# A fused attention and gated-convolution kernel: part of an output product moved ahead in the sixth chunk, the single tile's value product spread over two steps, and its convolution taps and gating moved later

## The chip, the cores and the metric

The kernel runs on one core of one Trainium2 chip. The metric is the device time in microseconds (us) of one execution; a kernel's time is the median of several. The engines are named as the profile names them: PE is the matmul engine (PEld its weight loads), DVE the vector engine, ACT the scalar engine, POOL GpSimd, SP the queue that issues most DMAs. Each works through its own instructions in order, and waits on semaphores for the others.

## The reference

Eight batches of 3200 rows with 256 features; z has 64. In short:

```python
scores = z @ z.T / S                    # per batch, S = 3200
attn = relu(scores) ** 2
x = u * (attn @ v)
gate = sigmoid(sum(conv_w[k] * x shifted down by 4 - k rows, k = 0..4))
out = (gate * (x @ w_val)) @ w_out
```

All in float32. The kernel splits each operand into a high part in the engine's reduced format and the rest, so that each product is three matmuls: low by high, high by low, high by high.

## The kernel before

**Tiles and steps.** A batch has 25 tiles of 128 rows: six chunks of four tiles (512 columns, `c` = 0 to 5 in the code, so the sixth chunk is `c` = 5) and a single tile at the end. The work of a batch is a list of 81 steps. A step takes one pair of key tiles for one chunk: its scores are computed three steps ahead on PE (`scores`, into a PSUM bank pair `s`), ACT squares them and casts the high part (`ah`, L643 to L646), DVE subtracts for the low part (`al`, L652), and then `attend` multiplies with v and adds into the chunk's two accumulator banks `acc`. Half of the pairs of scores are not computed but fetched, turned, from a copy in DRAM (`mirrored`, tile `m`). A chunk has 13 steps, the sixth has 16.

**Two row halves.** `side_by_side` (L426) runs two matmuls at once, each on 64 of PE's 128 rows, one writing bank 0 and the other bank 1. So a product is a list of pairs of matmuls, and it has two parts: in part 1 the halves change banks. At the start of part 1 `turn_round` puts a no-op on PE that waits for the last matmul of part 0, since the other half wrote these banks. `attend(…, 0)` and `attend(…, 1)` are the two parts of a step; scores or another product (a "fill") usually stand between them.

**Behind the attention.** When a chunk's last `attend` is done, DVE multiplies both `acc` banks with u (`gated`, L766, two instructions), which frees the banks for the next chunk. In the next chunk follow the convolution, the sigmoid, the value product (`value`, w_val, banks `misc0` and `misc1`), and one chunk later the output product (`project`, w_out, the same two `misc` banks, allocated anew each time, one buffer each). `project` stands at the first step of a chunk. In the sixth chunk its part 1 is cut into three pieces of two pairs: one in step 0, one each in steps 1 and 2.

**The single tiles.** They are handled in five groups of batches: (0, 1), (2, 3), (4, 5), (6), (7). In batches 0 to 7 their products with v (`swap`) fill steps of the sixth chunk. The rest of the work on the first four groups is put in the batch after the group, at step numbers counted from its start `s0`: taps of the convolution in `one_conv` (L1148 on ACT, L1150 on DVE), `one_sigmoid`, `one_value` (w_val, banks `misc0` and `misc1` too), `one_gated` (L1239, DVE reads both `misc` banks; two instructions), `one_gated_high` (L1243), `one_gated_low` (L1247), and at `s0` + 48 `one_project`. Step `s0` + 38 is the last of the third chunk, and step `s0` + 39 the first of the fourth.

**What sets the order.** The order is written by hand. For each step the loop at the end of the function issues PE's work, then, at a chunk's last step, `gated`, then what `at_step` put there, in the order of the calls. `fill_at` puts work between the two parts of a step.

Of the kernel before, what the change touches and what calls it, by code (L numbers as in the profile page):

```python
# [17 lines left out]
def attn_glu_kernel(  # L18
# [216 lines left out]
    def has_copy(b, c, i=None):  # L235


        if i is not None and place[b, c, i] >= NP - 2 and has_copy(b, c + 1):
            return False
        return c < n_chunks - 1 and b > 0  # L240
# [17 lines left out]
    def tiles(c, i):  # L258

        return (GROUP * i, GROUP) if c == ONE else pairs[i]  # L260
# [61 lines left out]
    def start(b, c):  # L322

        c = min(c, n_chunks - 1)
        return starts[b, c] if b < B else N
# [92 lines left out]
    def side_by_side(upper, lower):  # L418


        ins = None
        for i in range(max(len(upper), len(lower))):
            for r, mms in zip(rows, (upper, lower)):
                if i < len(mms):
                    out_, st, mv, first, last = mms[i]
                    ins = nc.tensor.matmul(out_, st[r], mv[r], start=first, stop=last)  # L426
        return ins
# [27 lines left out]
    def s_bank():  # L455

        if held_s[0] is None:
            next_s[0] = 1 - next_s[0]
            x = 1 - next_s[0]
        else:  # L460
            x = 1 - held_s[0]
        return ps.tile([P, 2, 512], F32, name=f"s{x}", bufs=1)

    def scores(b, c, i, terms=range(3)):
        if not terms:
            return
        k, n = tiles(c, i)
        w = sizes[c] * P
        if (b, c, i) not in st_:
            st_[b, c, i] = s_bank()  # L470
        s = st_[b, c, i]

        q = zt[b, c][:, :, :w].rearrange("p x (t a r) -> p x a t r", t=sizes[c], r=BLK)
        if has_copy(b, c, i):
            q = zq[b, c][:, :, :w].rearrange("p x (a y) -> p x a y", a=P // BLK)
        if halves(b, c, i):
            q, w = q[:, :, :, 2 * BLK :] if has_copy(b, c, i) else q[:, :, :, 2:], w // 2
        a = P // BLK
        sides = []
        for j in range(2):  # L480
            g, t = homes[k + (0 if n == 1 else j)]
            ks = slice(t * P, (t + 1) * P)
            qs = slice(j * (a // 2), (j + 1) * (a // 2)) if n == 1 else slice(0, a)
            kk = zt[b, g]
            mms = []
            for m in terms:
                kp, qp = (((0, 0), (0, 1), (1, 0)) if b == c == i == 0 else ((0, 1), (1, 0), (0, 0)))[m]
                mms.append((s[:, j, : w // 2 if n == 1 else w], kk[:, kp, ks], q[:, qp, qs], m == 0, m == 2))
            if both(c, i):
                for m in terms:  # L490
                    kp, qp = ((0, 1), (1, 0), (0, 0))[m]
                    q1 = zt[b, ONE][:, qp, j * (P // 2) : (j + 1) * (P // 2)]
                    mms.append((s[:, j, w // 2 : w // 2 + P // 2], kk[:, kp, ks], q1, m == 0, m == 2))
            sides.append(mms)
        side_by_side(*sides)

    def both(c, i):
        return c == n_chunks - 1 and i == SINGLE
# [7 lines left out]
    def halves(b, c, i):  # L506
        return two_pairs(b, c) and i == own(c, 1)
# [452 lines left out]
    def project(b, c, part, piece=0, pieces=1):  # L960
        if part == piece == 0:
            pos[b, c] = [ps.tile([P, 512], F32, name=f"misc{x}", bufs=1) for x in range(DH)]
        sides = [project_list(b, c, x, part == 0, part == 1) for x in (part, 1 - part)]
        turn_round("misc", cut(sides, piece, pieces), part and piece == 0)
# [352 lines left out]
    def at_step(s, fn, *args, first=False):  # L1317
        work = todo.setdefault(min(s, END), [])
        work.insert(0 if first else len(work), (fn, args))

    def fill_at(s, fn, *args):
        filling.setdefault(s, []).append((fn, *args))
# [38 lines left out]
    )  # L1361
    V_HIGH = (7, 8, 9, 10, 11, 12, 13, 16, 17, 18, 14, 15, 19)

    CONVERSIONS = (
        (2, 2, convert_conv(), 10),
        (13, 4, convert("val"), 10 + 2 * LAG["val"]),
# [2 lines left out]
    for b in range(B):  # L1369
        for c in range(n_chunks + 1):  # L1370
            s0 = start(b, c)
# [23 lines left out]
            if (b, c) != LAST:  # L1395
# [7 lines left out]
                ends = project_places(nb, nc_)  # L1403
# [40 lines left out]
    for g, members in enumerate(GROUPS[:-1]):  # L1444
        s0 = start(members[-1] + 1, 0)
        at_step(s0 + 6, one_load, g)
        at_step(s0 + 9, one_mul, g)
        fill_at(s0 + 24, one_turn, g)
        at_step(s0 + 24, one_halo, g)
        at_step(s0 + 24, one_place, g)  # L1450
        at_step(s0 + 25, one_high, g)
        at_step(s0 + 26, one_low, g)
        for h in range(DH):
            for k in range(KW):
                at_step(s0 + 26 + 4 * h + max(k - 1, 0), one_conv, g, h, k)
        at_step(s0 + 34, one_sigmoid, g)
        for part in range(2):
            fill_at(s0 + 37, one_value, g, part)
        for e in range(DH):
            at_step(s0 + 37, one_gated, g, e)  # L1460
        at_step(s0 + 38, one_gated_high, g)
        at_step(s0 + 39, one_gated_low, g)
        for part in range(2):
            fill_at(s0 + 48 + part, one_project, g, part)
        at_step(s0 + 49, one_out, g)
    g, s0 = len(GROUPS) - 1, start(*LAST)
# [8 lines left out]
    at_step(9, fetch_weights, "out", w_out, "zq")  # L1475
    for first, step, fn, n in CONVERSIONS:
        for j in range(n + 1):
# [5 lines left out]
    with tc.manual_schedule():  # L1483
# [13 lines left out]
        for s in range(min(todo), END + 1):  # L1497
            b, c, i = steps[s] if s >= 0 else (0, 0, 0)
            cm, p = position(s)[1:] if s >= 0 else (0, s)
            ahead = steps[s + AHEAD] if 0 <= s + AHEAD < N and s != -1 else None  # L1500
            late = steps[AHEAD - 1] if s == 0 else None
            places, ends = (value_places(b, cm), project_places(b, cm)) if s >= 0 else ((), ())
            piece = PIECES[len(places)][places.index(p)] if p in places else None
            terms = [] if lacks(s) or not ahead else list(range(3))
            if s in FILL:
                no_wait(zeros[:, :P], zeros, "misc1", FILL[s])
            k = b * n_chunks + cm if s >= 0 else 0
            before = divmod(k - 2, n_chunks) if k >= 2 and p == project_at(b, cm) else None
# [3 lines left out]
            if s >= WHOLE_FROM:  # L1512
                assert not left and not terms and not piece and not before
                if s < END:
                    for h in range(DH):
                        attend_whole(b, c, i, h)
                        if s == WHOLE_FROM and h == 0:
                            one_turn(len(GROUPS) - 1)
            else:
                fill, whole = [], False  # L1520
                if before and ends:
                    project(*before, 0)
                    scores(*ahead, terms)
                    terms, fill = [], [(project, *before, 1, 0, len(ends) + 1)]
                elif before:
                    project(*before, 0)
                    scores(*ahead, terms[:1])
                    project(*before, 1)
                    terms = terms[1:]
                if p in ends:  # L1530
                    fill = [(project, *divmod(k - 2, n_chunks), 1, 1 + ends.index(p), len(ends) + 1)]
                if piece:
                    fill = [(value, *behind, *piece)]
                    behind = None
                fill += filling.get(s, [])
                if s >= NP and p == 0 and not before:

                    scores(*ahead, terms)
                    for h in range(DH):
                        attend_whole(b, c, i, h)  # L1540
                    terms, whole = (), True
                elif s >= 0 and c != ONE:
                    attend(b, c, i, 0)
                if late:
                    scores(*late)
                    attend(b, c, i, 1)
                    whole = True
                if s == -AHEAD:
                    scores(*ahead, terms)
                    z_turn(0, 1)  # L1550
                    terms = []
                if behind:
                    value(*behind, 0)
                if terms:
                    scores(*ahead, terms)
                for fn, *args in fill:
                    fn(*args)
                if s >= 0 and not whole and c != ONE:
                    left.append((b, c, i))
                if terms or fill or behind or s + 1 == WHOLE_FROM:  # L1560
                    for n in range(len(left)):
                        attend(*left.pop(0), 1, again=n > 0)
                if behind:
                    value(*behind, 1)
# [19 lines left out]
            if s == END:  # L1584

                b, c = LAST
                g = len(GROUPS) - 1
# [104 lines left out]
```

## Time and profile before

| | |
|---|---|
| time, median of 3 runs | 2253.08 us (2252.02 to 2254.63) |
| time of the profiled execution | 2252.91 us |
| its span, first to last instruction | 2251.1 us |
| PE busy | 2242.5 us, 100% of the span |
| DVE, ACT, POOL busy | 1855.5 us (82%), 1700.1 us (76%), 84.6 us (4%) |
| granted clock of PE | 1.00 |

The span is what the trace covers; the execution's own time has 1.8 us around it. An engine is counted as busy while an instruction runs on it, and matmul ends are modelled, so that PE's share is no measure of how densely matmuls start. The steps of a stretch are compared by the starts of their matmuls.

### The profile page before, as it was taken

Reading aid. Unit: us, or ns where it says so; the run is one execution under the profiler, and the core shown is the slowest. Engines: PE = TensorE matmul, PEld = TensorE weight load, DVE = VectorE, ACT = ScalarE, POOL = GpSimd, SP = SyncE. Lnnn points to the kernel's source line nnn. Section 1 sums busy time; section 2 is a strip of 40 time slices with the busy share of each in tenths; the row PEclk is TensorE's granted clock in tenths of the full one; section 3 lists DMA queues with packets and bytes.
Section 4 is the critical chain, followed back from the end, with each engine's and each line's share of the span. In section 5 each row is a group of like instructions: output and inputs, shape, how many; then the busy total and the mean of one; then the engine's idle time right before and its main releaser. Section 6 shows DMA issues by size and latency. Waiting matters only on the chain.

```text
span 2251.1 us, 49980 instructions
## 1 busy us (share of the span) xinstructions
PE 2242.5 (100%) x20283; PEld 1915.8 (85%) x20283; DVE 1855.5 (82%) x2290; ACT 1700.1 (76%) x2136; POOL 84.6 (4%) x128
## 2 busy tenths in 40 slices
PE   9999999999999999999999999999999999999999
PEld 7788988889888998888888889888888888988888
DVE  7988788877889778887888968888788887888777
ACT  8986688766887668876698766987669776697764
POOL 0000000000000000000000000000000000000001
PEclk9999999999999999999999999999999999999999
DMA  6558857887677876788777786778868778577663
GB/s 155 113 140 206 213 140 165 191 184 197 159 167 177 190 193 155 174 186 187 179 171 169 188 188 171 170 176 184 208 142 189 175 179 205 144 186 174 169 180 101
DMA packets 702423, 390.79 MB, mean 174 GB/s; under 512 B 410608, under 2 KB 635888, under 8 KB 702192
## 3 DMA queue, kind: packets, MB, share of 16 engines
q1 hardware_dynamic: 701376, 387.21, 73.1%
q8 instruction: 158, 2.59, 0.5%
q14 instruction: 73, 0.60, 0.1%
q10 hardware_dynamic: 816, 0.39, 0.1%
HBM read 213.92 MB, written 173.54 MB: 172 GB/s over the span
## 4 chain that ended last, share of the span: by engine, by line
PE 97%; DVE 2%; ACT 1%; issue 0%; DMA 0%; DVEq 0%; ACTq 0%
PE acc L426 71%; PE s L426 13%; PE misc L426 12%; DVE al L652 0%; DVE turned L518 0%; PE acc L736 0%; PE misc L731 0%; ACT a L643 0%; ACT a L644 0%; DVE gate L814 0%; PE acc L731 0%; DMA z_rows<-in_z_dram 0%; PE misc L201 0%; DVE x L766 0%; ACT ah L646 0%
## 5 line engine op out<-in xcount | busy, mean ns | idle before, releaser
L426 PE MATMUL acc<-ah,v_hl 64*128 64x512 f32 x9472 | 1610.2, 388 | 0.8 <-DVE x L766 0.7
L426 PEld LDWEIGHTS acc<-ah,v_hl 64*128 64x128 f32 x9472 | 948.0, 184 | 160.8 <-issue 1.9
L426 PE MATMUL acc<-al,v_hl 64*128 64x512 f32 x4736 | 968.1, 387 | 0.1
L426 PEld LDWEIGHTS acc<-al,v_hl 64*128 64x128 f32 x4736 | 483.9, 184 | 77.8 <-DVE al L652 1.3
L652 DVE TENSOR_TENSOR al<-a,ah 128x1024 fp32r<-128x1024 f32 x342 | 393.0, 1149 | 175.0 <-ACT ah L646 173.7
L643 ACT ACTIVATE a<-s 128x1024 f32<-128x1024 f32 x342 | 328.9, 962 | 132.0 <-PE s L426 118.8
L646 ACT CAST ah<-m 128x1024 fp32r<-128x1024 f32 x258 | 269.3, 1047 | 168.0 <-PE acc L426 90.9
L644 ACT ACTIVATE a<-a 128x1024 f32<-128x1024 f32 x342 | 343.5, 1004 | 10.8
L652 DVE TENSOR_TENSOR al<-m,ah 128x1024 fp32r<-128x1024 f32 x258 | 312.4, 1211 | 36.1 <-ACT ah L646 33.4
L646 ACT CAST ah<-a 128x1024 fp32r<-128x1024 f32 (+1 forms) x320 | 316.8, 990 | 10.2
L518 DVE STREAM_TRANSPOSE turned<-a 128x1024 f32<-128x1024 f32 (+1 forms) x282 | 323.1, 1146 | 0.2 <-DMA mir<-turned 0.2
L814 DVE SCALAR_TENSOR_TENSOR gate<-x,cw,gate 128x512 f32<-128x512 f32 (+1 forms) x392 | 285.4, 728 | 4.3 <-ACT gate L812 0.5
L426 PE MATMUL s<-zq,zhl 64*128 64x512 f32 (+1 forms) x1596 | 223.4, 378 | 0.0
L426 PEld LDWEIGHTS s<-zq,zhl 64*128 64x128 f32 x1596 | 154.6, 184 | 27.2
L766 DVE TENSOR_TENSOR x<-acc,ut 128x512 f32<-128x512 f32 (+1 forms) x96 | 61.4, 680 | 77.6 <-PE acc L426 64.7
L818 ACT ACTIVATE gate<-gate 128x512 f32<-128x512 f32 (+1 forms) x98 | 61.0, 622 | 65.7 <-DVE gate L814 65.3
L916 ACT CAST gvh<-gv 128x512 fp32r<-128x512 f32 x94 | 58.3, 620 | 50.2 <-DVE gv L912 49.6
L912 DVE TENSOR_TENSOR gv<-misc,gate 128x512 f32<-128x512 f32 x94 | 64.5, 686 | 21.2 <-PE misc L426 17.0
L426 PE MATMUL misc<-xh,w_val_lo 64*128 64x512 f32 x376 | 77.3, 387 | 0.1
L426 PE MATMUL misc<-xl,w_val_hi 64*128 64x512 f32 x376 | 77.2, 386 | 0.0
L426 PE MATMUL misc<-xh,w_val_hi 64*128 64x512 f32 x376 | 77.2, 386 | 0.0
L426 PE MATMUL s<-v_hl,ah 64*128 64x512 f32 x400 | 76.2, 394 | 0.0
(199 smaller groups left out, 2025.6 us busy)
## 6 DMA issues: line engine op xcount, KB each, us to landing
mir<-turned SPq DMA_DIRECT2D x468, 256.0 KB, 4.1
m<-mir SPq DMA_DIRECT2D x234, 512.0 KB, 5.0
u_raw<-in_u_dram SPq DMA_DIRECT2D x384, 64.0 KB, 3.7
mir<-turned SPq DMA_DIRECT2D x376, 64.0 KB, 2.3
m<-mir SPq DMA_DIRECT2D x94, 256.0 KB, 4.6
out_dram<-ob SPq DMA_DIRECT2D x152, 128.0 KB, 3.5
v_raws<-in_v_dram SPq DMA_DIRECT2D x100, 128.0 KB, 6.4
z_raw<-in_z_dram SPq DMA_DIRECT2D x180, 64.0 KB, 3.3
```

What stands on the lines that cost most here:

```text
L426: ins = nc.tensor.matmul(out_, st[r], mv[r], start=first, stop=last)
L518: nc.vector.transpose(into[:, t : t + m], a[:, j * w : (j + m) * w].rearrange("p (t m x) -> p t m x", t=m, x=BLK))
L643: nc.scalar.activation(a[:, : n * w].rearrange("p (j x) -> p j x", j=2), s[:, :, :each], AF.Relu, scale=scale)
L644: nc.scalar.activation(a, a, AF.Square)
L646: nc.scalar.copy(hi, a)
L652: nc.vector.tensor_tensor(lo, a, f32(hi), op=ALU.subtract)
L766: nc.vector.tensor_tensor(x[:, h, HALO + cols.start : HALO + cols.stop], accs[b, c][h][:, cols] if with_ is None else with_, ut[b, c][:, h ...
L814: nc.vector.scalar_tensor_tensor(g, tap, cw[:, h, k : k + 1], g, op0=ALU.mult, op1=ALU.add)
L818: nc.scalar.activation(g, g, AF.Sigmoid)
L912: nc.vector.tensor_tensor(gv[:, :w], pvs[b, c][e][:, :w], gates[b, c][:, e, :w], op=ALU.mult)
L916: nc.scalar.copy(gvs[b, c][0][:, e, :w], gv_[b, c, e][:, :w])
```

## The change

The output product's first piece of part 1 moves, in the sixth chunk, from between the two parts of the first `attend` to ahead of both. The single tile's value product, both parts at `s0` + 37, now has part 0 at `s0` + 37 and part 1 at `s0` + 38; `one_gated`, `one_gated_high` and `one_gated_low` move from 37, 38, 39 to 38, 39, 40. The taps stand at a table `ONE_CONV` of steps, and the sigmoid one step later.

```diff
--- before.py
+++ after.py
@@ -1360,6 +1360,8 @@
         (16, (18, 19, 24), None),
     )
     V_HIGH = (7, 8, 9, 10, 11, 12, 13, 16, 17, 18, 14, 15, 19)
+
+    ONE_CONV = ((0, 0, 1, 2, 4), (4, 5, 6, 7, 8))
 
     CONVERSIONS = (
         (2, 2, convert_conv(), 10),
@@ -1452,14 +1454,14 @@
         at_step(s0 + 26, one_low, g)
         for h in range(DH):
             for k in range(KW):
-                at_step(s0 + 26 + 4 * h + max(k - 1, 0), one_conv, g, h, k)
-        at_step(s0 + 34, one_sigmoid, g)
+                at_step(s0 + 26 + ONE_CONV[h][k], one_conv, g, h, k)
+        at_step(s0 + 35, one_sigmoid, g)
         for part in range(2):
-            fill_at(s0 + 37, one_value, g, part)
+            fill_at(s0 + 37 + part, one_value, g, part)
         for e in range(DH):
-            at_step(s0 + 37, one_gated, g, e)
-        at_step(s0 + 38, one_gated_high, g)
-        at_step(s0 + 39, one_gated_low, g)
+            at_step(s0 + 38, one_gated, g, e)
+        at_step(s0 + 39, one_gated_high, g)
+        at_step(s0 + 40, one_gated_low, g)
         for part in range(2):
             fill_at(s0 + 48 + part, one_project, g, part)
         at_step(s0 + 49, one_out, g)
@@ -1520,8 +1522,11 @@
                 fill, whole = [], False
                 if before and ends:
                     project(*before, 0)
-                    scores(*ahead, terms)
-                    terms, fill = [], [(project, *before, 1, 0, len(ends) + 1)]
+                    if terms:
+                        scores(*ahead, terms)
+                        terms, fill = [], [(project, *before, 1, 0, len(ends) + 1)]
+                    else:
+                        project(*before, 1, 0, len(ends) + 1)
                 elif before:
                     project(*before, 0)
                     scores(*ahead, terms[:1])
```

**The first step of the sixth chunk, PE** (batch 0; the other seven are alike). `misc` are the output product's banks, `acc` the accumulators that the product with v (`ah`, `al` by `v_hl`) fills, `s` the bank of `swap`. Before:

```order
L426 MATMUL misc_3380<-gvh,w_out_hi 128x512
L426 MATMUL acc_3393<-ah,v_hl_714 128x512 [waits DVE_49,Activation_49]
L426 MATMUL acc_3394<-ah,v_hl_714 128x512 [waits DVE_49]
L426 MATMUL acc_3393<-al,v_hl_714 128x512
L426 MATMUL acc_3394<-al,v_hl_714 128x512
L426 MATMUL acc_3393<-ah,v_hl_714 128x512
L426 MATMUL acc_3394<-ah,v_hl_714 128x512
L426 MATMUL misc_3380<-gvh,w_out_lo 128x512 [waits PE_49]
L426 MATMUL misc_3379<-gvh,w_out_lo 128x512
L426 MATMUL misc_3380<-gvl,w_out_hi 128x512
L426 MATMUL misc_3379<-gvl,w_out_hi 128x512
L426 MATMUL s_3406<-v_hl_714,ah 128x512 [waits PE_49]
```

After:

```order
L426 MATMUL misc_3380<-gvh,w_out_hi 128x512
L426 MATMUL misc_3380<-gvh,w_out_lo 128x512 [waits PE_49]
L426 MATMUL misc_3379<-gvh,w_out_lo 128x512
L426 MATMUL misc_3380<-gvl,w_out_hi 128x512
L426 MATMUL misc_3379<-gvl,w_out_hi 128x512
L426 MATMUL acc_3398<-ah,v_hl_714 128x512 [waits DVE_49,Activation_49]
L426 MATMUL acc_3399<-ah,v_hl_714 128x512 [waits DVE_49]
L426 MATMUL acc_3398<-al,v_hl_714 128x512
L426 MATMUL acc_3399<-al,v_hl_714 128x512
L426 MATMUL acc_3398<-ah,v_hl_714 128x512
L426 MATMUL acc_3399<-ah,v_hl_714 128x512
L426 MATMUL s_3406<-v_hl_714,ah 128x512 [waits PE_49]
```

The four matmuls of the first piece of part 1, with the wait for part 0 on PE itself, have moved ahead of the six of the first `attend` part, which wait for DVE.

**The end of the third chunk, DVE** (batch 2, where the first group's single tiles are handled). L528 is a transpose at the chunk's last steps, L1239 is `one_gated`, L766 is `gated`, L652 makes a low part of attention weights, L230 the low part of z. Before:

```order
L528 STREAM_TRANSPOSE turned<-a 128x8x32
L1239 TENSOR_TENSOR one_sum<-misc_9962,one_sum 128x256 [waits PE_49]
L1239 TENSOR_TENSOR one_sum<-misc_9963,one_sum 128x256
L766 TENSOR_TENSOR x<-acc_9408,ut 128x512 [waits PE_49,Pool_49]
L766 TENSOR_TENSOR x<-acc_9409,ut 128x512 [waits PE_49]
L652 TENSOR_TENSOR al<-m,ah 128x4x2x128 [waits DMAHW7_49,Activation_49]
L230 TENSOR_TENSOR zhl_9998<-zz,zhl_9998 128x512 [waits DVE_49]
L652 TENSOR_TENSOR al<-a,ah 128x1024 [waits Activation_49]
```

After:

```order
L528 STREAM_TRANSPOSE turned<-a 128x8x32
L766 TENSOR_TENSOR x<-acc_9408,ut 128x512 [waits PE_49,Pool_49]
L766 TENSOR_TENSOR x<-acc_9409,ut 128x512 [waits PE_49]
L652 TENSOR_TENSOR al<-m,ah 128x4x2x128 [waits DMAHW7_49,Activation_49]
L230 TENSOR_TENSOR zhl_9985<-zz,zhl_9985 128x512 [waits DVE_49]
L1239 TENSOR_TENSOR one_sum<-misc_9962,one_sum 128x256
L1239 TENSOR_TENSOR one_sum<-misc_9963,one_sum 128x256
L652 TENSOR_TENSOR al<-a,ah 128x1024 [waits Activation_49]
```

The two L1239 stood ahead of `gated` and stand now behind it, behind one L652 and behind L230. In batches 4 and 6 the rows are the same; in batch 7 there is no L230.

**The start of the fourth chunk, PE** (the same batch, after the change; before it the rows are the same but for buffer numbers). The last three rows of the third chunk's `acc` are shown, and the first two of the output product:

```order
L426 MATMUL acc_9409<-al,v_hl_7844 128x512
L426 MATMUL acc_9408<-ah,v_hl_7844 128x512
L426 MATMUL acc_9409<-ah,v_hl_7844 128x512
L426 MATMUL misc_10057<-gvh,w_out_lo 128x512 [waits DVE_49]
L426 MATMUL misc_10058<-gvh,w_out_lo 128x512 [waits DVE_49]
```

The output product's first matmul on each `misc` bank waits for DVE, as before; what has moved is the work on DVE for which it waits.

## Rows read from the trace of the kernel before

**Rows 1.** The page: span, busy time of the engines, and the chain of work that ended last, by engine.

```profile
span 2251.1 us, 49980 instructions
PE 2242.5 (100%) x20283; PEld 1915.8 (85%) x20283; DVE 1855.5 (82%) x2290; ACT 1700.1 (76%) x2136; POOL 84.6 (4%) x128
...
PE 97%; DVE 2%; ACT 1%; issue 0%; DMA 0%; DVEq 0%; ACTq 0%
```

**Rows 2.** Who waited for whom, of PE's weight loads, which carry the waits of the matmuls: waiting engine and line, releaser, us in total, times, longest.

```profile
PEld misc L426 <- PE misc L426: 1.2, 5, 0.3
PEld acc L426 <- DVE al L652: 1.3, 3, 0.5
...
PEld acc L426 <- DVE x L766: 1.1, 4, 0.3
```

**Rows 3.** Timeline around the start of the sixth chunk in batch 1, PE, its weight loads and DVE: start, duration, engine, line, operation, output and inputs, count (like neighbours are merged into one row), and in brackets the idle time before it and what ended it.

```profile
513.63 0.39 PE L426 MATMUL acc<-ah,v_hl 64*128 64x512 f32 x2
...
513.85 0.39 PE L426 MATMUL misc<-gvh,w_out_lo 64*128 64x512 f32 x2
...
514.13 1.29 DVE L766 TENSOR_TENSOR x<-acc,ut 128x512 f32<-128x512 f32 x2 [3.29 <-PE acc L426]
...
514.99 0.39 PE L426 MATMUL misc<-gvh,w_out_hi 64*128 64x512 f32 x2
...
515.56 0.50 PE L426 MATMUL acc<-ah,v_hl 64*128 64x512 f32 x2 [0.19 <-DVE x L766]
...
519.19 0.44 PE L426 MATMUL misc<-gvh,w_out_hi 64*128 64x512 f32 x2
```

**Rows 4.** The same place in batch 2.

```profile
794.06 0.39 PE L426 MATMUL misc<-gvh,w_out_lo 64*128 64x512 f32 x2
...
795.42 0.74 PE L426 MATMUL acc<-ah,v_hl 64*128 64x512 f32 x2
...
795.67 0.18 PEld L426 LDWEIGHTS acc<-ah,v_hl 64*128 64x128 f32 x1 [0.29 <-DVE x L766]
...
799.12 0.61 PE L426 MATMUL misc<-gvh,w_out_hi 64*128 64x512 f32 x2
```

**Rows 5.** Timeline of the value product of the single tiles of the first group (batch 2) and of the boundary of the third and fourth chunk behind it.

```profile
700.30 0.28 PE L426 MATMUL misc<-one_r,w_val_lo 64*128 64x256 f32 x2
...
700.77 0.40 PE L426 MATMUL misc<-one_r,w_val_hi 64*128 64x256 f32 x4
...
701.23 0.19 PEld L426 LDWEIGHTS misc<-one_r,w_val_lo 64*128 64x128 f32 x2 [0.27 <-PE misc L426]
...
701.46 0.40 PE L426 MATMUL misc<-one_r,w_val_hi 64*128 64x256 f32 x4
...
702.05 0.39 PE L426 MATMUL acc<-ah,v_hl 64*128 64x512 f32 x2
...
705.65 0.72 DVE L1239 TENSOR_TENSOR one_sum<-misc,one_sum 128x256 f32<-128x256 f32 x2
...
705.93 0.39 PE L426 MATMUL acc<-ah,v_hl 64*128 64x512 f32 x2
...
706.09 0.52 PEld L426 LDWEIGHTS misc<-gvh,w_out_lo 64*128 64x128 f32 x2 [0.19 <-DVE one_sum L1239]
706.16 0.76 PE L426 MATMUL misc<-gvh,w_out_lo 64*128 64x512 f32 x2
...
706.43 1.29 DVE L766 TENSOR_TENSOR x<-acc,ut 128x512 f32<-128x512 f32 x2
...
707.63 1.21 DVE L652 TENSOR_TENSOR al<-m,ah 128x1024 fp32r<-128x1024 f32 x1
...
708.77 0.68 DVE L230 TENSOR_TENSOR zhl<-zz,zhl 128x512 fp32r<-128x512 f32 x1
```

**Rows 6.** Timeline of DVE a little earlier in the same chunk: what follows an L230 without a gap, a tap (L1150) and an L652 behind it, and the place behind L912.

```profile
679.40 0.43 DVE L1150 SCALAR_TENSOR_TENSOR one_sum<-one_f,cw,one_sum 128x256 f32<-128x256 f32 x1
679.76 1.21 DVE L652 TENSOR_TENSOR al<-m,ah 128x1024 fp32r<-128x1024 f32 x1
...
693.87 0.68 DVE L230 TENSOR_TENSOR zhl<-zz,zhl 128x512 fp32r<-128x512 f32 x1
694.47 0.48 DVE L1150 SCALAR_TENSOR_TENSOR one_sum<-one_f,cw,one_sum 128x256 f32<-128x256 f32 x1
...
698.01 0.69 DVE L652 TENSOR_TENSOR al<-a,ah 128x512 fp32r<-128x512 f32 x1 [0.53 <-ACT ah L646]
```

**Rows 7.** Timeline of the same boundary in batch 7 (fourth group, one batch, so half as wide), PE and DVE.

```profile
2095.41 0.45 DVE L1239 TENSOR_TENSOR one_sum<-misc,one_sum 128x128 f32<-128x128 f32 x2
...
2097.36 0.39 PE L426 MATMUL acc<-ah,v_hl 64*128 64x512 f32 x2
...
2097.59 0.39 PE L426 MATMUL misc<-gvh,w_out_lo 64*128 64x512 f32 x2
...
2097.86 1.29 DVE L766 TENSOR_TENSOR x<-acc,ut 128x512 f32<-128x512 f32 x2 [2.01 <-PE acc L426]
...
2099.07 1.21 DVE L652 TENSOR_TENSOR al<-m,ah 128x1024 fp32r<-128x1024 f32 x1
...
2100.20 1.22 DVE L652 TENSOR_TENSOR al<-a,ah 128x1024 fp32r<-128x1024 f32 x1
```

**Rows 8.** Timeline of PE where scores of 256 columns, 0.35 us, stand between the two parts of an `attend`.

```profile
502.47 0.52 PE L426 MATMUL s<-zq,zhl 64*128 64x256 f32 x6
502.82 0.40 PE L426 MATMUL acc<-ah,v_hl 64*128 64x512 f32 x2
```

**Rows 9.** PE's pace at the start of the program (timeline), and a stretch at its end, behind the last matmul, by busy time: bounds, length, busy us of PE, PEld, DVE, ACT, POOL with counts, granted clock, DMA share, GB/s.

```profile
8.96 0.79 PE L426 MATMUL s<-zhl 64*128 64x512 f32 x2
12.39 0.40 PE L426 MATMUL acc<-al,v_hl 64*128 64x512 f32 x2
...
2246.90:2251.10 4.20, 0.00 (x0) 0.00 (x0) 0.40 (x1) 0.00 (x0) 0.00 (x0) 1.00 0.70 233
```

## The prediction

> **What bounds the kernel now.** I read the page first. PE is busy for 2242.5 of 2251.1 us, and 97% of the chain that ended last is PE [rows 1]. So a change is worth what it adds to or takes from PE's waits, and work on DVE, ACT or SP counts only where PE stands still for it. Second I read who waited for whom at PE's weight loads [rows 2]. Three rows touch this change: PE waiting for itself ahead of `misc` matmuls (1.2 us in 5 waits, the longest 0.3), for the low part of weights (1.3 us in 3), and for `gated` ahead of `acc` (1.1 us in 4). Those are totals over the program, and small: there is not much to be had. Third I read timelines at the places the order names: the start of the sixth chunk [rows 3, 4], the single tile's value product and the chunk boundary behind it [rows 5, 7], and the taps [rows 6].
>
> A unit for what follows: pairs of 512-column matmuls start 0.228 us apart where nothing is late (513.85 to 514.99 us is five of them) [rows 3].
>
> **Part one, the output product's piece (eight places).** From the first output-product pair to the first pair of the next piece there are 6 + 3 + 2 pairs, a `swap` that is worth 1.5, then 3 and 6 pairs of `acc`: 21.5 pairs, 4.90 us undisturbed. In batch 1 it takes 513.85 to 519.19, 5.34 us: 0.44 us are lost, because both `acc` matmuls wait until DVE has read both banks (L766 runs from 514.13 for 1.29 us, to 515.42; PE would have been ready at 515.22 and starts at 515.56) [rows 3]. In batch 2 the halves stand in the other order. The leading half goes ahead at 795.42, the other waits and starts 0.25 us later; the leading half arrives at the next piece after 5.06 us, 0.16 late, and the one behind 0.25 later than that, 0.41 [rows 4]. I count the half behind, since the next turn waits for both. Batches 1, 3, 5, 7 against 0, 2, 4, 6: 4 x 0.44 + 4 x 0.41 = 3.4 us lost now.
>
> The change puts two pairs, 0.46 us, ahead of the wait. They cover it: PE would reach `acc` after 515.9, DVE is done at 515.42. But part 1 of the product now stands straight behind part 0, and its no-op waits for part 0's last matmul, which until now had the `acc` pairs to cover it. What such a bare turn costs is seen in the value product of the single tiles, where both parts stand back to back: pairs of 256 columns are 0.1175 us apart (700.30 to 700.77 is four), so its 12 pairs should take 1.41 us, and they take 1.75, to 702.05 [rows 5]. Of the 0.34 us, 0.23 is the gap ahead of 701.23, and 0.11 the second pair, which starts 0.23 behind the first instead of 0.12. I take 0.34 for 512 columns too, eight times, 2.7 us. Net gain of part one: 3.4 - 2.7 = 0.7 us. Its bounds: nothing for the turn (gain 3.4), and twice the row (loss 2.0). What follows has the `swap` alone, 0.34 us, between the two `acc` parts; scores of 0.35 us between such parts cost nothing (502.47 to 502.82) [rows 8], so I take nothing here.
>
> **Part two, the value product and its gating (four places).** Parts 0 and 1 now stand in different steps with `acc` pairs between them, so the bare turn goes: 0.34 us each in batches 2, 4, 6, and about 0.2 in batch 7, where the matmuls are half as wide (an estimate from the 0.23 gap; there is no row for it).
>
> But with part 1 in the chunk's last step, `one_gated` also moves there, and in DVE's order it comes behind `gated`, the next L652 and (but in batch 7) L230. The output product at the start of the next chunk takes the same two `misc` banks, one buffer each, so PE cannot begin it until both L1239 have read them. Already before, it had to wait a little: L1239 ran from 705.65 for 0.72 us, and the output product's weight load waited 0.19 us for it [rows 5]. Now DVE cannot start L766 before the chunk's last `acc` pair is done, so everything in front of L1239 is work that PE watches:
>
> - The last `acc` pair started at 705.93 and comes 0.34 earlier, 705.59. L766 starts 0.50 behind it, as in the three boundaries shown (513.63 to 514.13, 705.93 to 706.43, 2097.36 to 2097.86) [rows 3, 5, 7]: 706.09.
> - Both L766: 1.20 (706.43 to 707.63). L652: 1.14 (707.63 to 708.77) [rows 5]. L230: 0.60 (693.87 to 694.47) [rows 6]. Both L1239: 0.72 [rows 5]. Ends at 709.75.
> - Before, the second L1239 ended at 706.37. PE waited for it then and waits for it now, so what stands behind it on PE is 3.38 us later. Three times: 10.1 us. The turn that is gone is already in this, since the chain starts from 705.59.
> - Batch 7: 2097.36 less 0.2, plus 0.50, 1.21 (2097.86 to 2099.07), 1.13 (2099.07 to 2100.20), and 0.45 for the narrower L1239, ends at 2100.45. The output product started at 2097.59 without a wait [rows 7]. 2.9 us, and 0.1 for the late second pair: 3.0.
>
> Sum of part two: 13.1 us slower. Behind the stalled product on PE stand that chunk's scores and `acc` pairs, and ACT waits for the scores; PE itself needs these three steps later, so I see no second stall. `one_gated_high` and `one_gated_low` are off PE's path: the product that reads them is at step 48.
>
> **Part three, the taps.** From the step at 679.40 one tap (0.36 us of DVE until the L652 behind it) goes away, one is added five steps later, behind L912, where DVE stood idle for 0.53 us waiting for ACT ahead of 698.01 [rows 6]. Nothing on PE waited at the first place, and the second is covered. Were that cover gone, L652 would come 0.4 us late, with `attend` three steps behind it. The three waits for low parts of weights [rows 2] would give at most 1.3 us if the moved tap were in front of them; I take zero.
>
> **Sum.** 2252.91 (the profiled execution) + 13.1 - 0.7 = 2265.3. The median of the runs is 0.17 above that execution, so 2265.4.
>
> **The rivals.**
>
> - *PE's clock falls in the new waits.* PE would stand still for some 3.5 us, from 705.98 (705.59 and a matmul of 0.39) to the end of the first L1239 at about 709.4. At the program's start two matmuls of a pair took 0.79 us at 8.96 and 0.40 at 12.39, so a slow stretch of 3.4 us costs half of that, 1.7. If each of the four waits brought one, 6.8 more: 2272. Against it: behind the last matmul PE does nothing for 4.20 us and the granted clock stays at 1.00, its 2.4 GHz level [rows 9]. Chance 0.08. The Trainium skill's page "TensorE: Matmul & The Clock Gate", section "HAM oscillation — how this bites in real kernels", describes just such a kernel, whose matmul engine waits for data in every round and starts each at half clock. By that rule this rival would be the likeliest; the trace's idle stretch at full granted clock does not agree with it, though no wait of this length between matmuls is in the trace before.
> - *The turn of 512-column parts is dearer than that of 256.* At 0.68 instead of 0.34, part one loses 2.0 instead of gaining 0.7: 2268.0. For it: the engine drains longer matmuls. Against it: the gap in the row is a latency behind a matmul's end. Chance 0.07.
> - *Part of the loss comes back.* While PE stands still, DVE and ACT get ahead, and the waits for low parts behind it would shrink. At most the 1.3 us of rows 2: 2264. Chance 0.06.
> - *The output product finds its banks free (not slower).* If DVE had `one_gated` done by the chunk's end, only the gains were left: 3 x 0.34 + 0.2 + 0.7 = 1.9, and 2251.0. It has the time for it, since part 1 of the value product ends a whole `attend` part ahead of the chunk's end. It decides when the four waits come below 1.9 / 4 = 0.5 us each. Against it stands the order of DVE, where L1239 is behind both L766, and the wait for L1239 in the row of before [rows 5]. Chance 0.04.
>
> **How the numbers follow.** The forecast has 0.75. A measurement of this kernel can tell about 0.2%, 4.5 us, from no change. The range runs from 2262.6 (part one's turn free, 2252.91 + 13.1 - 3.4), taken a little lower for shorter DVE chains, to 2268.0 (the dear turn) and a part of the clock rival: 2262 to 2269. Outside lie most of the clock rival, the free banks, and what I have not thought of. Slower by over 0.2%: 0.94; within: 0.04, which is the free banks; faster: 0.02.
>
> **What would show it.** In the profile after: at the start of the fourth chunk in batches 2, 4, 6, 7 PE's weight loads wait for DVE L1239 by about 3.4 us (in all some 13 us under that releaser, where there were 0.2), with L766, L652 and L230 running in the meantime. At the sixth chunk the waits for L766 are gone, and eight short waits of PE for itself ahead of `misc` have come. The four at the value product are gone. The granted clock stays at 1.00. The prediction is wrong if L1239 runs ahead of L766, if PE starts the output product while L1239 is still to come, or if the pairs behind a stall are 0.4 us apart.

## The result, and the profile after

The changed kernel takes 2272.77 us (median of 5 runs, 2272.26 to 2273.90) against 2253.08 us (5 runs, 2252.02 to 2254.63): ratio 1.0089, 95% interval 1.0079 to 1.0100. It is slower, as forecast, but by 19.7 us and not by 12.3, and it lies above the range of 2262 to 2269.

The page of the kernel after, as in [rows 1]: span, busy time, and the chain of work that ended last.

```profile
span 2270.8 us, 49978 instructions
...
PE 2249.0 (99%) x20283; PEld 1889.8 (83%) x20283; DVE 1854.8 (82%) x2290; ACT 1700.6 (75%) x2136; POOL 85.7 (4%) x128
...
PE 97%; DVE 2%; ACT 1%; issue 1%; DMA 0%; DVEq 0%; ACTq 0%
```

PE has the same 20283 matmuls and is busy for 6.5 us longer, in a span 19.7 us longer. So some of the loss is waiting, and some is matmuls that take longer. The mean granted clock of the run is 0.996, where before it was 1.000.

Who waited for whom in the kernel after, PE first and then its weight loads (us in total, times, longest), against [rows 2]:

```profile
PE misc L426 <- DVE one_sum L1239: 13.7, 4, 3.9
```

```profile
PEld misc L426 <- DVE one_sum L1239: 15.4, 4, 4.3
PEld misc L426 <- PE misc L426: 5.1, 16, 0.5
PEld acc L426 <- DVE al L652: 1.3, 3, 0.5
```

The wait for L766 ahead of `acc` (1.1 us before) is gone. Weight loads wait for PE itself 16 times (5 before): eight are the turns of the moved piece, about 0.49 us each, and eight, 0.15 us each, stand ahead of another output product, where one stood before; the four at the value product are gone. PE stands still four times for L1239, 13.7 us in all. What the change does to the order is as the prediction had it. The place in batch 2, timeline of PE and DVE (start, duration, engine, line, operation, in brackets the idle time before it and what ended it), answers to [rows 5]:

```profile
704.82 0.39 PE L426 MATMUL acc<-ah,v_hl 64*128 64x512 f32 x2
...
705.31 1.29 DVE L766 TENSOR_TENSOR x<-acc,ut 128x512 f32<-128x512 f32 x2 [0.64 <-PE acc L426]
...
706.52 1.21 DVE L652 TENSOR_TENSOR al<-m,ah 128x1024 fp32r<-128x1024 f32 x1
...
707.65 0.68 DVE L230 TENSOR_TENSOR zhl<-zz,zhl 128x512 fp32r<-128x512 f32 x1
...
708.25 0.75 DVE L1239 TENSOR_TENSOR one_sum<-misc,one_sum 128x256 f32<-128x256 f32 x2
...
708.72 0.83 PE L426 MATMUL misc<-gvh,w_out_lo 64*128 64x512 f32 x2 [3.52 <-DVE one_sum L1239]
...
711.76 1.04 PE L426 MATMUL acc<-ah,v_hl 64*128 64x512 f32 x2
712.19 1.04 PE L426 MATMUL acc<-al,v_hl 64*128 64x512 f32 x2
```

From the start of the last `acc` pair to the end of the second L1239 it is 709.00 - 704.82 = 4.18 us; the prediction had 4.16. But the last two rows are pairs 0.43 us apart, where they should be 0.228. That was named as a sign that the prediction is wrong. Stretches of the same place by busy time (bounds, length, busy us of PE, PEld, DVE, ACT, POOL with counts, granted clock, DMA share, GB/s), and of batch 6:

```profile
705.20:708.70 3.50, 0.01 (x2) 0.00 (x0) 3.39 (x6) 3.44 (x4) 1.05 (x1) 1.00 0.62 131
708.70:710.10 1.40, 1.38 (x11) 1.05 (x13) 1.40 (x3) 0.75 (x2) 0.00 (x0) 1.00 1.16 302
710.10:713.50 3.40, 3.40 (x20) 2.65 (x18) 1.18 (x2) 1.05 (x2) 0.00 (x0) 0.50 0.34 50
713.50:717.00 3.50, 3.50 (x34) 3.19 (x32) 1.35 (x2) 3.27 (x4) 0.00 (x0) 1.00 0.00 0
...
1829.70:1836.50 6.80, 5.87 (x27) 5.75 (x29) 3.49 (x5) 2.34 (x4) 0.00 (x0) 0.50 0.56 113
```

In batch 2 the clock stays at 1.00, the 2.4 GHz level, through the whole wait and for 1.4 us in which PE is at work again. Then it is at 0.50, the 1.2 GHz level, for 3.4 us: 20 matmuls start there, against 34 in the 3.5 us behind it. In batch 6 the slow stretch lasts 6.8 us, and 27 matmuls start in it. The waits of batches 4, 6 and 7 on PE's timeline (for batch 6 with the last pair ahead of it), and stretches in batch 4 and batch 7:

```profile
1269.97 1.12 PE L426 MATMUL misc<-gvh,w_out_lo 64*128 64x512 f32 x2 [3.87 <-DVE one_sum L1239]
...
1826.72 0.39 PE L426 MATMUL acc<-ah,v_hl 64*128 64x512 f32 x2
...
1830.63 1.12 PE L426 MATMUL misc<-gvh,w_out_lo 64*128 64x512 f32 x2 [3.52 <-DVE one_sum L1239]
...
2115.51 0.69 PE L426 MATMUL misc<-gvh,w_out_lo 64*128 64x512 f32 x2 [2.79 <-DVE one_sum L1239]
```

```profile
1269.80:1270.30 0.50, 0.33 (x1) 0.28 (x1) 0.50 (x3) 0.00 (x0) 0.00 (x0) 0.59 1.00 326
...
1273.00:1273.50 0.50, 0.50 (x6) 0.49 (x5) 0.00 (x0) 0.00 (x0) 0.00 (x0) 0.69 0.01 1
...
2116.40:2119.80 3.40, 3.40 (x20) 3.11 (x18) 1.54 (x2) 0.42 (x1) 0.00 (x0) 0.50 0.00 0
```

In batch 4 the clock falls as PE comes back (a mean of 0.59 over 1269.80 to 1270.30) and is up again at about 1273.3 (0.69 over 1273.00 to 1273.50); in batch 6 it has fallen, at 1829.7, before PE is back at 1830.63; in batch 7 it falls 0.9 us behind PE's return. All four places have a slow stretch.

### The profile page after: what moved, and what is told of

It reads as the page before. It is cut to its first block, busy times and chain, and to the rows that moved or that the text cites. A ratio compares the mean times of both kernels' runs of the same rounds, so it can differ in the third digit from the quotient of the medians.

```text
span 2270.8 us, 49978 instructions
## 1 busy us (share of the span) xinstructions
PE 2249.0 (99%) x20283; PEld 1889.8 (83%) x20283; DVE 1854.8 (82%) x2290; ACT 1700.6 (75%) x2136; POOL 85.7 (4%) x128
## 4 chain that ended last, share of the span: by engine, by line
PE 97%; DVE 2%; ACT 1%; issue 1%; DMA 0%; DVEq 0%; ACTq 0%
PE acc L426 70%; PE s L426 13%; PE misc L426 12%; DVE al L652 1%; DVE turned L518 0%; PE acc L736 0%; PE misc L731 0%; ACT a L643 0%; ACT a L644 0%; DVE gate L814 0%; PE acc L731 0%; DMA z_rows<-in_z_dram 0%; DVE x L766 0%; ACT ah L646 0%; PE s L866 0%
## 5 line engine op out<-in xcount | busy, mean ns | idle before, releaser
L426 PE MATMUL acc<-ah,v_hl 64*128 64x512 f32 x9472 | 1590.3, 388 | 0.1
L426 PEld LDWEIGHTS acc<-ah,v_hl 64*128 64x128 f32 x9472 | 923.9, 184 | 171.5 <-issue 0.9
L426 PE MATMUL acc<-al,v_hl 64*128 64x512 f32 x4736 | 949.2, 387 | 0.1
L652 DVE TENSOR_TENSOR al<-a,ah 128x1024 fp32r<-128x1024 f32 x342 | 393.2, 1150 | 192.1 <-ACT ah L646 191.3
L426 PEld LDWEIGHTS acc<-al,v_hl 64*128 64x128 f32 x4736 | 468.4, 185 | 85.0 <-DVE al L652 1.3
L652 DVE TENSOR_TENSOR al<-m,ah 128x1024 fp32r<-128x1024 f32 x258 | 312.5, 1211 | 35.0 <-ACT ah L646 32.4
L766 DVE TENSOR_TENSOR x<-acc,ut 128x512 f32<-128x512 f32 (+1 forms) x96 | 61.4, 681 | 79.9 <-PE acc L426 67.3
L912 DVE TENSOR_TENSOR gv<-misc,gate 128x512 f32<-128x512 f32 x94 | 64.5, 686 | 21.2 <-PE misc L426 16.9
L426 PE MATMUL misc<-gvh,w_out_lo 64*128 64x512 f32 x304 | 66.3, 403 | 14.2 <-DVE one_sum L1239 13.7
```

What stands on the lines that cost most here:

```text
L652: nc.vector.tensor_tensor(lo, a, f32(hi), op=ALU.subtract)
L766: nc.vector.tensor_tensor(x[:, h, HALO + cols.start : HALO + cols.stop], accs[b, c][h][:, cols] if with_ is None else with_, ut[b, c][:, h ...
L912: nc.vector.tensor_tensor(gv[:, :w], pvs[b, c][e][:, :w], gates[b, c][:, e, :w], op=ALU.mult)
```

## The experiments

All were timed beside the kernel before on the same chip: 2252.78 us for e1 to e4, and 2253.15 us for e5 to e8.

**Each part alone.** e1 is the kernel before with part one only:

```diff
-                    scores(*ahead, terms)
-                    terms, fill = [], [(project, *before, 1, 0, len(ends) + 1)]
+                    if terms:
+                        scores(*ahead, terms)
+                        terms, fill = [], [(project, *before, 1, 0, len(ends) + 1)]
+                    else:
+                        project(*before, 1, 0, len(ends) + 1)
```

> The kernel before with part one alone: the output product's first piece of part 1 ahead of the first attend of the sixth chunk. Prediction on record: 3.4 us of waits gone, 2.7 us of bare turns come, 2252.4. Rival, by the trace of the changed kernel: the bare turn and what it leaves between the two halves costs 0.40 us until the next piece, as much as the wait it replaces, so no difference, 2253.0 within 0.5. If the turn of 512 columns cost twice that of 256: 2255.

Measured: 2252.76 us, ratio 1.0000 (0.9991 to 1.0009). Part one does nothing that can be told; a gain of 0.7 us, as forecast, would lie within that interval too.

e2 is the kernel before with the value product and its gating at their new steps:

```diff
-            fill_at(s0 + 37, one_value, g, part)
+            fill_at(s0 + 37 + part, one_value, g, part)
...
-            at_step(s0 + 37, one_gated, g, e)
-        at_step(s0 + 38, one_gated_high, g)
-        at_step(s0 + 39, one_gated_low, g)
+            at_step(s0 + 38, one_gated, g, e)
+        at_step(s0 + 39, one_gated_high, g)
+        at_step(s0 + 40, one_gated_low, g)
```

> The kernel before with part two alone: value product over steps 37 and 38, gating at 38 to 40, taps and sigmoid and the sixth chunk as before. Waits and clock theory: four waits for one_gated, 13.1 us, and about 7 us of matmuls at half clock behind them, 2273. If the piece of part one or the taps had a share in the loss, it would be missing here: 2270 or less. Granted clock below 1.00 four times.

Measured: 2273.42 us, ratio 1.0092 (1.0078 to 1.0105), with a mean clock of 0.996. The whole loss is in part two.

e3 is the kernel before with the taps and `one_sigmoid` at their new steps:

```diff
+    ONE_CONV = ((0, 0, 1, 2, 4), (4, 5, 6, 7, 8))
...
-                at_step(s0 + 26 + 4 * h + max(k - 1, 0), one_conv, g, h, k)
-        at_step(s0 + 34, one_sigmoid, g)
+                at_step(s0 + 26 + ONE_CONV[h][k], one_conv, g, h, k)
+        at_step(s0 + 35, one_sigmoid, g)
```

> The kernel before with the taps and the sigmoid at their new steps alone. Both theories: no difference, 2253.0 within 0.5. A rival by which the moved tap helps the low parts of weights ahead of it: at most 1.3 us faster, 2251.8.

Measured: 2252.00 us, ratio 0.9997 (0.9987 to 1.0006). Part three is worth nothing that the times can tell. They do not exclude the 1.3 us of the rival, but the trace speaks against it: PE's weight loads wait for L652 for 1.4 us in 3 waits in e3, against 1.3 us in 3 before [rows 2].

**The wait taken away.** e4 is the changed kernel with `one_gated` issued ahead of `gated` in the third chunk's last step; nothing else differs from the changed kernel:

```diff
+                for fn, args in [w for w in todo.get(s, ()) if w[0] is one_gated]:
+                    todo[s].remove((fn, args))
+                    fn(*args)
                 for h in range(DH):
                     gated(b, cm, h)
```

> The changed kernel with one thing different: in the last step of the third chunk one_gated is issued ahead of gated, so that DVE does both L1239 before it waits for the chunk's end. If the waits for one_gated are the whole cause, and the clock falls only because of them: all 20 us are gone, clock 1.00, and the bare turns at the value product too, 2252.0 (0.2 to 0.3 us gained at three places, since DVE then ends L1239 some 0.57 us behind the start of the last acc pair). If something else in the change lowers the clock: above 2258.

Measured: 2251.56 us, ratio 0.9996 (0.9987 to 1.0005), clock 1.000. The place in batch 2, timeline of e4:

```profile
705.74 0.71 DVE L1239 TENSOR_TENSOR one_sum<-misc,one_sum 128x256 f32<-128x256 f32 x2
...
706.18 0.51 PEld L426 LDWEIGHTS misc<-gvh,w_out_lo 64*128 64x128 f32 x2 [0.27 <-DVE one_sum L1239]
...
706.45 1.29 DVE L766 TENSOR_TENSOR x<-acc,ut 128x512 f32<-128x512 f32 x2
```

DVE now reads the banks at about the time that PE comes to them: a weight load waits 0.27 us for L1239, and no matmul of PE does, where PE waited 3.52 us. The place of two instructions in DVE's order is the cause of all 20 us, waits and clock together.

**The wait kept, PE kept busy.** e5 is the changed kernel with matmuls of no use in the wait, 14 of 512 columns (11 in batch 7), into a free score bank:

```diff
+    busy = {start(m[-1] + 1, 0) + 39: 14 if len(m) == 2 else 11 for m in GROUPS[:-1]}
...
+                if s in busy:
+                    bank = ps.tile([P, 2, 512], F32, name=f"s{next_s[0]}", bufs=1)
+                    w_hi = weights["val"][0]
+                    for _ in range(busy[s]):
+                        nc.tensor.matmul(
+                            bank[:, 0], w_hi[:, 0, :P], w_hi.rearrange("p h d -> p (h d)"), start=True, stop=True
+                        )
```

> The changed kernel with 14 (in batch 7: 11) matmuls of 512 columns that nobody reads put on PE between the third chunk's end and the output product, into a free score bank: PE is busy for 3.2 us of each of the four waits, and the waits are as long as they were. Waits and clock theory: the clock stays at 1.00, and only the waits of 13.1 us are left, 2265.5. If the half clock in the records costs nothing, or the waits and what follows from them are the whole loss: 2272 to 2273.

Measured: 2266.16 us (4 runs, 2265.35 to 2267.83), ratio 1.0058 (1.0044 to 1.0072), clock 1.000. Timeline of PE, and two stretches of e5 with the columns given above:

```profile
705.17 0.39 PE L426 MATMUL acc<-ah,v_hl 64*128 64x512 f32 x2
705.49 3.49 PE L1528 MATMUL s<-w_val_hi 128*128 128x512 f32 x14
709.07 0.83 PE L426 MATMUL misc<-gvh,w_out_lo 64*128 64x512 f32 x2
```

```profile
705.40:709.40 4.00, 3.90 (x17) 2.73 (x15) 3.74 (x7) 3.14 (x4) 1.05 (x1) 1.00 0.65 131
709.40:713.40 4.00, 4.00 (x37) 3.57 (x38) 2.23 (x2) 2.22 (x3) 0.00 (x0) 1.00 0.63 132
```

The output product starts 3.90 us behind the last `acc` pair (709.07 - 705.17), exactly as in the kernel after (708.72 - 704.82), so the time until DVE frees the banks is unchanged; but behind it 37 matmuls start in 4.0 us at a clock of 1.00. The waits alone cost 2266.16 - 2253.15 = 13.0 us (parts one and three are in this run too, and e1 and e3 show nothing for them). What is left to the kernel after, 2272.77 - 2266.16 = 6.6 us, is the clock.

**The wait shortened.** e6 is the changed kernel with the same three lines as in e4, but behind the loop of `gated`, so that L1239 waits for both L766 but no longer for L652 and L230.

> The changed kernel with one_gated on DVE directly behind gated, ahead of L652 and L230: DVE's chain behind the last acc pair is 0.50 + 1.20 + 0.72 us instead of 4.2, so the waits are about 1.7 us each, 6.8 in all instead of 13.1. If the clock stays at full for a wait of 1.7 us: 2259.6. If it falls for such a wait as well and costs as much as in the changed kernel: 2266 to 2267.

Measured: 2262.97 us, ratio 1.0043 (1.0029 to 1.0057), between the two. Waits of PE, and stretches behind the waits in batches 2, 4 and 7 of e6:

```profile
PE misc L426 <- DVE one_sum L1239: 7.3, 4, 2.1
```

```profile
708.00:712.00 4.00, 4.00 (x38) 3.42 (x36) 2.90 (x4) 2.98 (x4) 0.00 (x0) 1.00 0.78 173
1265.60:1269.10 3.50, 3.50 (x20) 2.72 (x18) 3.21 (x4) 0.98 (x2) 0.00 (x0) 0.51 0.97 198
2105.30:2108.80 3.50, 3.50 (x20) 3.33 (x18) 3.03 (x3) 0.60 (x2) 0.00 (x0) 0.51 0.21 73
```

Waits of about 2 us brought a fall at two places (batches 4 and 7) and none at the other two (batches 2 and 6). What decides between them stays open. The fall in batch 4 stands behind the longest of the four waits, but the one in batch 7 behind the shortest, as the timeline of PE in these two batches shows. The number of falls does not seem to be fixed either: the mean clock of the four executions of e6 goes from 0.997 to 0.999.

```profile
1264.50 0.82 PE L426 MATMUL misc<-gvh,w_out_lo 64*128 64x512 f32 x2 [2.13 <-DVE one_sum L1239]
...
2104.76 0.69 PE L426 MATMUL misc<-gvh,w_out_lo 64*128 64x512 f32 x2 [1.66 <-DVE one_sum L1239]
```

**Parts one and two done otherwise.** e7 is the kernel before; in the first step of the sixth chunk the `swap` goes ahead of both `acc` parts, and the output product's piece stays between them:

```diff
                     project(*before, 0)
-                    scores(*ahead, terms)
+                    if terms:
+                        scores(*ahead, terms)
+                    else:
+                        for fn, *args in filling.pop(s, []):
+                            fn(*args)
                     terms, fill = [], [(project, *before, 1, 0, len(ends) + 1)]
```

> The kernel before with another filling of the same wait: in the first step of the sixth chunk swap goes ahead of the first attend part, between part 0 of the output product and acc, and the piece of part 1 stays between the two attend parts. 0.34 us of work cover the wait for gated, and no turn stands bare: swap and acc are between the product's parts, the piece between acc's parts. Expected gain 0.41 to 0.44 us at eight places, 2249.7. If the bare turn was not what ate part one's gain: no better than the piece alone, 2252.5.

Measured: 2249.64 us, ratio 0.9985 (0.9977 to 0.9994), faster than the kernel before.

e8 is e7 with the value product one step earlier, its gating as before:

```diff
-            fill_at(s0 + 37, one_value, g, part)
+            fill_at(s0 + 36 + part, one_value, g, part)
```

> e7_swap_between and the value product of the single tiles over steps 36 and 37, with the gating at 37 to 39 as before, and the old taps: the bare turn is gone without moving one_gated behind gated. Expected: 3.4 us from the swap, and 0.2 us at three places and 0.2 in batch 7 from the turns (DVE's L1239 doesn't come earlier, so that a part of the 0.34 goes into waiting for it): 2248.9. If PE waits at step 36 for the misc banks that the chunk's own value product holds: above 2250.

Measured: 2248.90 us, ratio 0.9980 (0.9971 to 0.9989). It is faster than the kernel before and the changed one. Between e7 and e8 the runs can't tell (their intervals overlap), though the difference, 0.7 us, is near the 0.8 that was expected. In e8's trace no weight load waits for PE at the value product any more; for L1239 they wait 1.4 us in 3 waits.

## Why the prediction was wrong, point by point

- **The waits for L1239: right.** 13.1 us predicted, 13.0 measured (e5), four waits of 3.9 us or less, behind the rows that were named. With e2 and e4 it is shown that they, and the clock with them, are the whole loss.
- **The clock: wrong, and this is the step that failed.** The sum had nothing for it. The mechanism stood among the rivals with its price (6.8 us, 2272) and had a chance of 0.08; measured were 6.6 us (e5 against the kernel after) and 2272.77. That is most of the 7.4 us between forecast and result. The rest, 0.8 us, is what e5 lies above the forecast; it fits the 0.7 us that part one was to gain, and is within the scatter of e5's runs. It was marked down on one row, the end of the program in [rows 9]: 4.20 us without a matmul at a granted clock of 1.00. That stretch ends with the program, and the kernel after shows how far a fall can lag behind the last matmul. The last matmul on its timeline, and two stretches behind it:

```profile
2266.26 0.28 PE L1202 MATMUL s<-w_out_hi,one_r 128*128 128x256 f32 x1
```

```profile
2266.60:2269.90 3.30, 0.00 (x0) 0.00 (x0) 0.40 (x1) 0.00 (x0) 0.00 (x0) 1.00 0.89 298
2270.00:2270.80 0.80, 0.00 (x0) 0.00 (x0) 0.00 (x0) 0.00 (x0) 0.00 (x0) 0.50 0.00 0
```

  The same idle end that was read as "no fall" brings one here, 3.5 us after the last matmul (2266.54 to 2270.0). It does so in e3 too, which differs from the kernel before by the taps and the sigmoid alone; its last matmul starts at 2245.16 and takes 0.28 us, and these are two stretches from there on:

```profile
2245.30:2249.10 3.80, 0.14 (x2) 0.00 (x0) 0.42 (x1) 0.00 (x0) 0.00 (x0) 1.00 0.83 276
2249.20:2249.70 0.50, 0.00 (x0) 0.00 (x0) 0.00 (x0) 0.00 (x0) 0.00 (x0) 0.50 0.00 0
```

  In batch 2 of the kernel after it came 4.9 us after PE stopped (705.21 to 710.10), longer than the 4.20 us of [rows 9]. So that row could not exclude it: the record stopped too early. I should have weighed it as silent. Then the rule that I cited, of the Trainium skill's page "TensorE: Matmul & The Clock Gate", section "HAM oscillation — how this bites in real kernels", by which a matmul engine that waits for data in every round starts each at half clock, was the only thing that spoke on the question. This trace agrees with it in that all four rounds brought a fall, but only in batches 4 and 6 does PE start again at half clock; in batches 2 and 7 the fall comes 1.4 and 0.9 us later.
- **What a fall costs: about right, and in part by luck.** 1.7 us each was half of 3.4 us, the distance of two rows at the program's start. These rows do not show how long a slow stretch lasts. Two others of the kernel before, from PE's timeline there:

```profile
6.05 1.94 PE L426 MATMUL s<-zhl 64*128 64x512 f32 x6 [0.25 <-ACT zhl L225]
...
13.30 0.89 PE L426 MATMUL s<-zhl,zhl 64*128 64x512 f32 x6
```

  Six matmuls took 1.94 us at 6.05 already, against 0.89 later, so the slow pace had lasted longer than the 3.4 us; and the granted clock reads 1.00 there (6.00 to 12.00), so that the record doesn't show it as a slow stretch of the clock. But in the kernel after three of the four slow stretches do last about 3.4 us, and the fourth 6.8. By half of the time that PE was busy in them they come to 8.0 us (1.7 three times, and (1836.50 - 1830.63) / 2 = 2.9), against 6.6 measured. The runs of e5 alone span 2.5 us, so the difference may be scatter; it wasn't pursued.
- **Part one: the terms right, the sum too good.** The waits lost now were put at 3.4 us; e7, which removes them and adds no bare turn, gains 3.5. The turn was put at 0.34. Timeline of the kernel after in batch 1, against [rows 3]:

```profile
513.13 0.39 PE L426 MATMUL misc<-gvh,w_out_lo 64*128 64x512 f32 x2
...
514.26 0.39 PE L426 MATMUL misc<-gvh,w_out_hi 64*128 64x512 f32 x2
...
514.71 0.19 PEld L426 LDWEIGHTS misc<-gvh,w_out_lo 64*128 64x128 f32 x2 [0.49 <-PE misc L426]
514.71 0.50 PE L426 MATMUL misc<-gvh,w_out_lo 64*128 64x512 f32 x2
...
515.05 0.40 PE L426 MATMUL misc<-gvl,w_out_hi 64*128 64x512 f32 x2
...
518.42 0.39 PE L426 MATMUL misc<-gvh,w_out_hi 64*128 64x512 f32 x2
```

  514.26 to 514.71 is 0.45 instead of 0.23, and 514.71 to 515.05 is 0.34: 0.33 lost, as from parts of 256 columns, so the rival of the dear turn falls; the weight loads' waits at the other seven places, 0.48 or 0.49 us, are the same. But the next output-product piece comes at 518.42, 5.29 us behind the first pair where 4.90 are undisturbed: 0.39 lost, and 0.44 before. Some 0.06 go in the pairs that follow the turn, which the sum didn't count. So this place gains 0.05; at eight such places that is 0.4 us, an estimate, below what e1's interval can tell. In e7 the same stretch has no gap; timeline of its batch 1:

```profile
513.18 0.39 PE L426 MATMUL misc<-gvh,w_out_lo 64*128 64x512 f32 x2
...
514.54 0.39 PE L426 MATMUL s<-v_hl,ah 64*128 64x512 f32 x2
...
514.88 0.41 PE L426 MATMUL acc<-ah,v_hl 64*128 64x512 f32 x2
...
515.59 0.40 PE L426 MATMUL misc<-gvh,w_out_lo 64*128 64x512 f32 x2
...
518.12 0.39 PE L426 MATMUL misc<-gvh,w_out_hi 64*128 64x512 f32 x2
```

  From 513.18 to 518.12 it is 4.94 us. The `swap`, 0.34 us from 514.54 to 514.88, covers the last of DVE's read, and the `acc` pairs still cover the turn.
- **Part three: right**, at zero as far as e3 can tell.
- **The remaining rivals.** Nothing of the loss came back: L652's waits are 1.3 us before and after [rows 2]. The banks were not free; e4 is what that rival described, near its price (2251.0, measured 2251.56).

## What to carry to other kernels

Before an instruction that frees a buffer is put into a later step, look at what stands ahead of it on its own engine: here two reads of 0.4 us were put behind 2.9 us of other work (705.31 to 708.25), and the engine that bounds the kernel watched. A stall of that engine is not over when its wait ends, so price a possible fall of its clock into every wait of some us that a change opens (here it came behind waits of 1.66 to 3.87 us), and do not take an idle stretch that ends with the program as evidence that the clock holds. Where a wait on the bound engine needs cover, choose work that doesn't bring a drain of its own: the `swap` (e7) gained what the output product's piece (e1) gave away at its turn.

## What the runs showed of the hardware

- The clock's fall lags behind the stop, and by no fixed time: 2.6 us in batch 6 (the last pair there started at 1826.72 and took 0.39 us; the fall is at 1829.7), 3.5 at the program's end, 4.9 in batch 2 of the kernel after. So a fall can lie wholly behind the wait that brought it, where PE looks fully busy.
- The same kind of wait has different consequences. Four waits of 2.8 to 3.9 us (kernel after) had a fall each time, one of them for 6.8 us instead of 3.4; four of 1.7 to 2.1 us (e6) had two; those of 0.3 us (e4) had none. The long stretch isn't tied to its place: in e2, with the same waits of 3.87 us in batch 4 and 3.52 in batch 6, it is batch 4 that has it (0.50 from 1270.7 to 1277.4), and not batch 6.
- Matmuls of no use hold the clock: 14 of them, 3.49 us, in each wait (11 in batch 7) left it at 1.00 (e5), and were worth 6.6 us although the output product started as late.
